# One of a step's three score maxima computed in two parts of 256 keys, one in either half of TensorE's array

## The chip, the cores and the metric

The kernel runs on one core of one Trainium2 chip. The metric is the device time of one execution in microseconds (us). Three runs of the kernel before the change took 1636.03, 1638.93 and 1639.0 us (median 1638.93). One further execution was profiled; every duration of an instruction below is from it.

Engines: TensorE (PE for its matmuls, PEld for its weight loads), VectorE (DVE), ScalarE (ACT), GpSimd (POOL), and SyncE (SP), which issues DMAs. Each takes its instructions in order from a queue of its own; across engines, semaphores order them. TensorE writes to PSUM, which has eight banks of 128 x 512 float32.

## The reference

Two attention layers over the same shapes, their outputs side by side. S = 2048 positions, D = 576, 32 heads of 18.

```python
def _B_ref(x, wqkv, wo):                      # full attention
    qkv = (x @ wqkv).reshape(B, S, 3, H, Dh).transpose(2, 0, 3, 1, 4)
    q, k, v = qkv[0], qkv[1], qkv[2]
    scores = einsum("bhqd,bhkd->bhqk", q, k) * Dh ** -0.5
    o = einsum("bhqk,bhkd->bhqd", softmax(scores), v)
    return o.transpose(0, 2, 1, 3).reshape(B, S, D) @ wo

def _A_ref(x, wqkv, wo):                      # each query sees 8 keys: itself, 2, 4, ... 14 back
    ...
    logits = where(mask, einsum("bhsd,bhswd->bhsw", q, kg) * Dh ** -0.5, -1e9)
    o = einsum("bhsw,bhswd->bhsd", softmax(logits), vg)
    return o.transpose(0, 2, 1, 3).reshape(B, S, D) @ wo

return concatenate([a, b], axis=-1)           # a = _A_ref, b = _B_ref
```

## The kernel before

**Attention B** takes nearly all of TensorE's time. The heads are worked in eight groups of four (`g`), the queries of a group in four blocks of 512 (`b`), the keys of a block in 16 tiles of 128 (`kt`). One (g, b, kt) is a *step*: 32 blocks x 16 = 512 steps. In a step `score` (L222) makes, for each of the four heads, the 128 x 512 scores of the key tile against the block's queries (a matmul, L229, over 56 rows) and lets ScalarE take their exponential out of PSUM into `e` (L235). One step later `weigh` (L697) multiplies the four `e` by the values (L700, eight passes in the trace) into `po`, one bank that gathers a block's 16 steps. Heads 0 and 2 have their queries and keys on partitions 0 to 63 (r = 0, the lower rows of TensorE's array), heads 1 and 3 on partitions 64 to 127 (r = 1, the upper rows). Matmuls in the two halves can run at the same time.

**The maxima.** The softmax subtracts each query's largest score. It comes in as two further rows of `qs`, hence 56 rows in L229, so a block's maxima must be known before its steps begin. They are made as a second product, over 54 rows with the queries as weights: `take` (L156) multiplies 128 queries by 512 keys into a bank (L159), `reduce` (L163) has VectorE reduce that bank to one column of `mx` (L166). A block needs 64 such pieces: 2 halves `r`, 2 heads `p` in each, 4 query tiles `t`, 4 key ranges `k`. When the last one is reduced, `least` (L170) reduces over `k` (L173), and `turn`, `halve` and `place` follow in later steps: a transposition on VectorE, a split on POOL (L104 and L105), DMAs into `qs`. The maxima of block n + 1 and later are made during the steps of block n: a block's maxima last about 21 steps. `maximum(r)` (L208) hands out the next piece of half `r`. Pieces of the first eight blocks are mostly made earlier, while the projections run (`stream`, L286).

**Order in a step.** `score` is called for h = 0, 1, 2, 3; with `also` true, a piece of the other half (1 - r) is issued behind the score's matmul and its reduction behind the exponential. `positions` picks the heads that get one: three as a rule, four where `behind()` finds the maxima late. With heads 0, 1 and 2 the queue of TensorE is: score r0, maximum r1, score r1, maximum r0, score r0, maximum r1, score r1, then the weighing. `inside` holds products of output projections (`sums_of_a`, `quarter`) that go in front of the third or fourth score; `beside` (L991), which makes them, also takes two pieces of maxima along while there are any.

**Banks.** Seven banks besides `po`: four in the ring "scores", three in the ring "else" (L80), from which the maxima take theirs in turn.

**Attention A** is made on POOL, between the steps, in eight chunks of 256 queries (`local`, L814). A dictionary `agenda` holds what is due at which step; chunk j's plan begins at step 10 + 54 j (L1086). Counted from there, the products `match` (L837, L841) are due at 5, 7, 10, 12, ... 25, the maximum over the window on VectorE (L855) at 31 to 33, `lower` (L861) at 33, the exponential on ScalarE (L864) at 35, sums and reciprocals on VectorE (L855, L871) at 36 to 39, `share` (L874) at 39, the weighted sums (L880 to L883) at 39, 41, 44, ... 59, then L887 at 60 and L892 at 61. Each `match` or weighted sum holds POOL for about 4.6 us. POOL also does the end of each of attention B's blocks (`finish`, L705: L736, L737, L738 at 18, 19 and 20 steps behind its end). What is due at the end of a step is put into the engines' queues there; each engine gets to it when it can.

Of the kernel before, what the change touches and what calls it, by code (L numbers as in the profile page):

```python
# [7 lines left out]
F32 = mybir.dt.float32  # L8
# [3 lines left out]
ALU = mybir.AluOpType  # L12
AX = mybir.AxisListType
# [9 lines left out]
NG = H // 4  # L23
NT = S // 128
NB = S // 512
SCALE = DH ** -0.5
MASKED = -1e9 / SCALE
LEAST = -3.0e38
AB = 256
NJ = S // AB  # L30
SUB = AB // 4
# [5 lines left out]
PIECES = 2 * 4 * NB  # L37
# [4 lines left out]
AHEAD = 7  # L42
# [9 lines left out]
def ap(t, *dims):  # L52

    return bass.AP(tensor=t.tensor, offset=t.offset, ap=[list(t.ap[0])] + [list(d) for d in dims])
# [8 lines left out]
def two_attentions(ctx: ExitStack, tc, xa, wa, woa, xb, wb, wob, out):  # L63
# [5 lines left out]
    nc = tc.nc  # L69
# [5 lines left out]
    maxes = ctx.enter_context(tc.tile_pool(name="maxes", bufs=1))  # L75
# [33 lines left out]
    step = 0  # L109

    def later(n, f):
        agenda[step + n].append(f)
# [5 lines left out]
    def due():  # L118
        for f in agenda.pop(step, []):
            f()  # L120
# [29 lines left out]
    def block(g, b):  # L150

        qs, ks = sets[g % 3]
        mx = maxes.tile([128, 2, 2, 4, NB], F32, name="mx", bufs=3)
        left = 2 * PIECES

        def take(r, t, k, p):  # L156
            ps = bank()
            at = slice(64 * r, 64 * r + 54)
            nc.tensor.matmul(ps, qs[at, b, p, 128 * t : 128 * t + 128],  # L159
                             ks[at, p, 512 * k : 512 * k + 512], start=True, stop=True)  # L160
            return ps

        def reduce(ps, r, t, k, p):  # L163
            nonlocal left
            left -= 1
            nc.vector.tensor_reduce(mx[:, r, p, t, k : k + 1], ps, axis=AX.X, op=ALU.max)  # L166
            if left == 0:
                least()

        def least():  # L170
            m = least_rooms[n_least[0] % 2]
            n_least[0] += 1
            nc.vector.tensor_reduce(m[:, :16], mx.rearrange("q r p t k -> q (r p t) k"), axis=AX.X, op=ALU.max,  # L173
                                    negate=True)
            later(1, lambda: turn(m))

        def turn(m):

            raw = maxes.tile([128, 32], F32, name="mt", bufs=2)
            nc.vector.transpose(raw, m)  # L180
            later(1, lambda: halve(raw))

        def halve(raw):
            mh = maxes.tile([128, 32], F32R, name="mh", bufs=2)
            split_on(nc.gpsimd, mh, raw.bitcast(F32R), raw)
            later(2 if g == NG - 1 else 5, lambda: place(mh, raw))

        def place(*parts):
            placed.add((g, b))
            for k, t in enumerate(parts):  # L190
                for j in range(4):
                    load(ap(qs.bitcast(F32)[54 + k : 128 : 64, b, 0, 32 * j :], (128, 8), (1, 32)),
                         t.bitcast(F32)[32 * j : 32 * j + 16])

        return take, reduce


# [6 lines left out]
    blocks = {}  # L204
    given = [0, 0]
    projecting = True

    def maximum(r):  # L208

        n, i = divmod(given[r], PIECES)  # L210
        given[r] += 1
        if n not in blocks:
            blocks[n] = block(*divmod(n, NB))
        take, reduce = blocks[n]
        piece = (r, i // 2 // NB, i // 2 % NB, i % 2)
        ps = take(*piece)
        return lambda: reduce(ps, *piece)

    e_room = None
    counted = [-1]  # L220

    def score(g, b, kt, h, also, kind="scores"):  # L222

        assert (g, b) in placed
        qs, ks = sets[g % 3]
        p, r = divmod(h, 2)
        ps = bank(kind)
        at = slice(64 * r, 64 * r + 56)
        nc.tensor.matmul(ps, ks[at, p, 128 * kt : 128 * kt + 128], qs[at, b, p], start=True, stop=True)  # L229
        reduce = maximum(1 - r) if also else None  # L230

        counted[0] += 1
        early = counted[0] % 8 < 6
        e = (e_room if early else work).tile([128, 512], F32, name="e", bufs=6 if early else 2)
        nc.scalar.activation(e, ps, AF.Exp, scale=SCALE)  # L235
        if reduce:
            reduce()
        return e

    vs = {}  # L240
# [45 lines left out]
    def stream(products, most, last):  # L286
# [9 lines left out]
        for j in range(len(products)):  # L296
# [42 lines left out]
    with (tc.tile_pool(name="x", bufs=1, side="right") as xp,  # L339
# [103 lines left out]
        if True:  # L443
# [34 lines left out]
            for c in range(5):  # L478
                one, other = (load, nc.scalar.dma_start) if c % 2 == 0 else (nc.scalar.dma_start, load)
# [11 lines left out]
            ahead = deque()  # L491
# [67 lines left out]
            for t in range(NT):  # L559
                ps = bank()  # L560
# [78 lines left out]
            for k in range(2, 14):  # L639
                n = 46 if k == 2 else 36 + 4 * k  # L640
# [14 lines left out]
            for t in order[:4]:  # L655
                ps = bank()
# [18 lines left out]
            for c, b in order:  # L675
                n = min(128, 3 * D - 128 * c)
                work_list.append(((b % 2, ws[c][0], xas[b][0], slice(0, n), every),
                                  lambda ps, n=n: ps[:n], lambda ps, c=c, b=b, n=n: leave_a(c, b, n, ps)))

            es = []  # L680
            few = 2 * (NT - 4)
            turns = len(work_list) - NT + 4
            stream(work_list, lambda j: 2 * (j + 1) if j < NT - 4 else
                   few + (EARLY_PAIRS - few) * (j - NT + 5) // turns,
                   [[lambda h=h: es.append(score(0, 0, 0, h, False, "else")) for h in (r, r + 2)] for r in range(2)])
        wa_room.close()

        over, agenda = agenda, defaultdict(list)
# [2 lines left out]
        step = 0  # L691
# [5 lines left out]
    def weigh(*steps):  # L697
        for g, b, kt, es in steps:
            for i in range(4):
                nc.tensor.matmul(po[32 * i : 32 * i + 19], vs[g][:, kt, 19 * i : 19 * i + 19], es[i],  # L700
                                 start=kt == 0, stop=kt == NT - 1)
        if kt == NT - 1:
            finish(g, b)
# [86 lines left out]
    producing = set()  # L790
# [196 lines left out]
    inside = []  # L987
# [115 lines left out]

    total = early + rest

    def behind():

        most = 0
        for n in range(sum(given) // (2 * PIECES), NG * NB):
            until = NT * n - AHEAD  # L1110
            more = 3 * (until - step) + 2 * sum(step <= p < until for p in producing)
            most = max(most, 2 * PIECES * (n + 1) - sum(given) - more)
        return most

    def positions(n):

        if n == 3:
            ahead = given[1] > given[0]
            return (0, 1, 3) if ahead else (0, 1, 2)
        if n == 1:  # L1120
            return (0,) if given[0] > given[1] else (1,)
        return range(4) if n > 3 else (0, 1) if n == 2 else ()

    paired = False
    due()
    step += 1
    while step < ALL:
        n, kt = divmod(step, NT)
        g, b = divmod(n, NB)
        places = positions(min(4 if behind() > 0 else 3, total - sum(given)))  # L1130
        es = []
        for h in range(4):

            if inside and h == (3 if 3 in places else 2):
                inside.pop(0)()
            es.append(score(g, b, kt, h, h in places))
        for fs in (behind_scores, outside):
            while fs:
                fs.pop(0)()

        paired = paired or kt % 2 == 0 and sum(given) == total
        for _ in range(1 if paired and step < ALL - 2 else len(waiting)):
            if waiting:
                waiting.pop(0)()
        if ready and (kt % 2 == 0 or not paired):
            weigh(ready.pop(0))
        ready.append((g, b, kt, es))
        if paired and kt % 2:
            weigh(*ready)
            ready.clear()  # L1150
        due()

        if len(waiting) > (0 if not paired else 2 if kt % 2 else len(waiting)):
            waiting.pop(0)()
        step += 1
# [24 lines left out]
```

## Time and profile before

| | us |
|---|---|
| median of three runs | 1638.93 |
| lowest, highest | 1636.03, 1639.0 |
| the profiled execution | 1637.69 |
| its span, first to last instruction | 1635.9 |

| engine | busy us | share of the span | instructions |
|---|---|---|---|
| TensorE, matmuls | 1627.4 | 99% | 12906 |
| TensorE, weight loads | 944.2 | 58% | 12906 |
| VectorE | 1393.1 | 85% | 2366 |
| ScalarE | 1223.1 | 75% | 2419 |
| POOL | 959.4 | 59% | 792 |

The costliest groups are the maxima's reductions (L166, 2048 of 684 ns), the exponentials (L235, 2048 of 608 ns), the maxima's matmuls (L159, 2048 of 422 ns), the scores' matmuls (L229, 2048 of 425 ns) and the weighing (L700, 4096 passes of 599 ns). A row of the timeline has the start in us from the span's start, the duration in us (from the first to the last of merged instructions), engine, line, operation, what is written and read by the program's names, the shapes and a count; in square brackets stands the idle time of the engine before it and what ended it. Matmuls overlap, so their durations do not add up; their starts are what to read. In a row of windows stand, for each engine, the busy time and number of instructions, then the granted TensorE clock (1.00 is full speed), and the share and rate of the DMA engines.

### The profile page before, as it was taken

How to read it: one execution, taken by the hardware profiler on the slowest of the kernel's cores; microseconds unless marked ns; L12 is line 12 of the kernel's file. 1: busy time of each engine (PE TensorE's matmuls, PEld its weight loads, DVE VectorE, ACT ScalarE, POOL GpSimd, SP SyncE). 2: the span in 40 equal slices, each digit the busy share in tenths (PEclk: the TensorE clock that was granted, in tenths of full speed). 3: DMA queues.
4: the chain of work that ended last, by engine and by line, in shares of the span. 5: the costliest groups of instructions: out<-in, count | busy, mean ns of one | idle time of the engine just before them, and what ended most of it. 6: DMA issues, size and time to landing. Idle time of an engine off the chain costs nothing.

```text
span 1635.9 us, 33786 instructions
## 1 busy us (share of the span) xinstructions
PE 1627.4 (99%) x12906; PEld 944.2 (58%) x12906; DVE 1393.1 (85%) x2366; ACT 1223.1 (75%) x2419; POOL 959.4 (59%) x792
## 2 busy tenths in 40 slices
PE   9999999999999999999999999999999999999998
PEld 7999888999433344444444444444444444444676
DVE  5199999999889899889889989899899899888533
ACT  6324432111899999999999999999999999998554
POOL 2306642210365996995994995995995997920000
PEclk9999999999999999999999999999999999999999
DMA  8937955522222253163135235332532151033201
GB/s 251 237 117 201 270 159 141 136 87 91 46 57 65 73 141 81 34 147 93 48 86 146 55 109 116 82 90 62 120 104 58 51 139 47 21 122 126 99 38 59
DMA packets 186050, 172.01 MB, mean 105 GB/s; under 512 B 119152, under 2 KB 132976, under 8 KB 184160
## 3 DMA queue, kind: packets, MB, share of 16 engines
q1 hardware_dynamic: 181024, 158.31, 34.9%
q0 software_dynamic: 4032, 10.63, 3.2%
q8 instruction: 101, 1.65, 0.5%
q10 hardware_dynamic: 832, 0.92, 0.2%
q14 instruction: 61, 0.50, 0.1%
HBM read 96.94 MB, written 71.90 MB: 103 GB/s over the span
## 4 chain that ended last, share of the span: by engine, by line
PE 96%; DMA 1%; POOL 1%; DVE 1%; issue 0%; ACT 0%; SPq 0%; POOLq 0%; ACTq 0%; DVEq 0%
PE po L700 31%; PE bank L229 25%; PE bank L322 14%; PE bank L159 14%; PE bank L1005 7%; PE bank L259 5%; DMA dqk<-olo 1%; POOL xlo L370 1%; PE bank L474 0%; DMA more<-xa 0%; DVE mx L166 0%; POOL olo L462 0%; DMA out<-y 0%; PE bank L980 0%; ACT vs L540 0%
## 5 line engine op out<-in xcount | busy, mean ns | idle before, releaser
L166 DVE TENSOR_REDUCE mx<-bank 128x1 f32<-128x512 f32 x2048 | 1288.1, 684 | 140.5 <-PE bank L159 113.3
L235 ACT ACTIVATE e<-bank 128x512 f32<-128x512 f32 x2048 | 1061.7, 608 | 87.1 <-PE bank L229 52.4
L159 PE MATMUL bank<-ks,qs 54*128 54x512 f32 x2048 | 750.5, 422 | 0.7 <-DVE mx L166 0.5
L229 PEld LDWEIGHTS bank<-qs,ks 56*128 56x128 f32 x2048 | 327.6, 185 | 446.5 <-ACT e L235 418.5
L229 PE MATMUL bank<-qs,ks 56*128 56x512 f32 x2048 | 571.3, 425 | 0.0
L700 PE MATMUL po<-e,v 128*19 128x512 f32 x4096 | 537.4, 599 | 0.0
L159 PEld LDWEIGHTS bank<-ks,qs 54*128 54x128 f32 x2048 | 340.1, 184 | 11.3 <-DVE mx L166 4.0
L700 PEld LDWEIGHTS po<-e,v 128*19 128x19 f32 x4096 | 70.6, 97 | 184.9 <-issue 182.1
L837 POOL TENSOR_TENSOR pr<-aq,akv 128x1024 f32<-128x1024 f32 x72 | 158.4, 2200 | 16.1 <-DMA akv<-da 13.5
L880 POOL TENSOR_TENSOR pr<-lg,akv 128x1024 f32<-128x1024 f32 x72 | 158.2, 2197 | 0.6
L841 POOL TENSOR_TENSOR pr<-pr 128x1024 f32<-128x1024 f32 x64 | 152.4, 2382 | 5.0
L650 ACT ACTIVATE ohi<-bank 128x512 f32<-128x512 f32 (+1 forms) x56 | 30.4, 595 | 151.0 <-issue 99.4
L322 PE MATMUL bank<-xhi,ahi 64*128 64x512 f32 (+1 forms) x448 | 114.6, 387 | 0.0
L322 PE MATMUL bank<-xhi,alo 64*128 64x512 f32 (+1 forms) x448 | 111.3, 387 | 0.0
L322 PE MATMUL bank<-xlo,ahi 64*128 64x512 f32 (+1 forms) x448 | 109.1, 388 | 0.1
L881 POOL TENSOR_TENSOR pr<-pr 128x512 f32<-128x512 f32 x72 | 92.3, 1283 | 5.6
L370 POOL TENSOR_TENSOR alo<-raw,ahi 128x512 fp32r<-128x512 f32 (+1 forms) x14 | 17.6, 1256 | 120.6 <-ACT ahi L369 93.7
L462 POOL TENSOR_TENSOR olo<-olo,ohi 128x512 fp32r<-128x512 f32 x36 | 46.1, 1294 | 66.3 <-ACT ohi L461 60.5
L736 POOL TENSOR_TENSOR o<-o,rec 128x512 f32<-128x512 f32 x29 | 37.4, 1289 | 59.7 <-ACT e L235 24.9
L322 PEld LDWEIGHTS bank<-xhi,ahi 64*128 64x128 f32 (+1 forms) x448 | 64.9, 181 | 3.0
L322 PEld LDWEIGHTS bank<-xhi,alo 64*128 64x128 f32 (+1 forms) x448 | 62.2, 182 | 2.9
L1005 PE MATMUL bank<-wohi,at 64*128 64x288 f32 x512 | 63.8, 295 | 0.0
(197 smaller groups left out, 1784.0 us busy)
## 6 DMA issues: line engine op xcount, KB each, us to landing
do<-n SPq DMA_DIRECT2D x28, 512.0 KB
da<-ohi SPq DMA_DIRECT2D x52, 256.0 KB
akv<-da SPq DMA_DIRECT2D x64, 175.5 KB
out<-y SPq DMA_DIRECT2D x32, 288.0 KB
qs<-dqk SPq DMA_DIRECT2D x30, 288.0 KB
ks<-dqk SPq DMA_DIRECT2D x30, 288.0 KB
at<-dao SPq DMA_DIRECT2D x64, 128.0 KB
rec<-drec SPq DMA_DIRECT2D x29, 256.0 KB
```

The source lines that it names most:

```text
L159: nc.tensor.matmul(ps, qs[at, b, p, 128 * t : 128 * t + 128], ks[at, p, 512 * k : 512 * k + 512], start=True, stop=True)
L166: nc.vector.tensor_reduce(mx[:, r, p, t, k : k + 1], ps, axis=AX.X, op=ALU.max)
L229: nc.tensor.matmul(ps, ks[at, p, 128 * kt : 128 * kt + 128], qs[at, b, p], start=True, stop=True)
L235: nc.scalar.activation(e, ps, AF.Exp, scale=SCALE)
L259: nc.tensor.matmul(ps, a, b, start=c == i == 0, stop=c == 4 and i == 1)
L322: nc.tensor.matmul(ps, a, b, start=start, stop=stop)
L700: nc.tensor.matmul(po[32 * i : 32 * i + 19], vs[g][:, kt, 19 * i : 19 * i + 19], es[i], start=kt == 0, stop=kt == NT - 1)
L837: nc.gpsimd.tensor_mul(pr, ap(st["q"][:, 2 * c], (SUB, 2), (0, W), (1, SUB)), window(st["k"], c))
L841: nc.gpsimd.tensor_add(st["pr"], st["pr"], pr)
L880: nc.gpsimd.tensor_mul(at, ap(st["lg"], (0, 2), (SUB, W), (1, SUB)), window(st["v"], c))
L881: nc.gpsimd.tensor_add(at[:, :, :4], at[:, :, :4], at[:, :, 4:])
L1005: nc.tensor.matmul(ps, a, b, start=start, stop=stop)
```

## The change

Each step now issues two whole pieces and one half of two others. `parts_of_maximum` takes one piece of either half of the array with the same `p`, `t`, `k`. In one step it multiplies the first 256 keys of both, in the next step the last 256. Both products of a step go into one bank, the piece of r = 0 into columns 0 to 255, that of r = 1 into 256 to 511, and one reduction of two rows of 256 reads them. The matmul of r = 1 is issued at the step's start. ScalarE gets a nop that waits for it, and the matmul of r = 0 waits for the nop.

The scores are issued in the order h = 0, 2, 1, 3. TensorE's queue in a step is: part r1, score r0, maximum r1, score r0, score r1, part r0, score r1, maximum r0, then the weighing. The two whole pieces are reduced right after the exponentials of h = 0 and h = 3, the parts after that of h = 1. `behind` and `positions` are gone; the total number of pieces is the same.

`mx` has a last dimension of 2 for the two parts. A whole piece writes only the first of the two, so `mx` is set to the least float32 on POOL when a block's first piece is handed out, and `LEAST` is changed for that. The reduction in `least` goes over eight values instead of four. In the built program the block's first reduction on VectorE waits for POOL's memset. `inside` now always goes in front of the fourth score.

```diff
-LEAST = -3.0e38
+LEAST = -3.4028234e38
...
-        mx = maxes.tile([128, 2, 2, 4, NB], F32, name="mx", bufs=3)
+        mx = maxes.tile([128, 2, 2, 4, NB, 2], F32, name="mx", bufs=3)
+        nc.gpsimd.memset(mx, LEAST)
...
-        def take(r, t, k, p):
-            ps = bank()
+        def take(ps, r, t, k, p, part=None):
             at = slice(64 * r, 64 * r + 54)
-            nc.tensor.matmul(ps, qs[at, b, p, 128 * t : 128 * t + 128],
-                             ks[at, p, 512 * k : 512 * k + 512], start=True, stop=True)
-            return ps
+            first, n = (0, 512) if part is None else (256 * part, 256)
+            return nc.tensor.matmul(ps if part is None else ps[:, 256 * r : 256 * r + 256],
+                                    qs[at, b, p, 128 * t : 128 * t + 128],
+                                    ks[at, p, 512 * k + first : 512 * k + first + n], start=True, stop=True)
...
+            if part is None:
+                ins = nc.vector.tensor_reduce(mx[:, r, p, t, k, :1], ps, axis=AX.X, op=ALU.max)
+            else:
+                ins = nc.vector.tensor_reduce(mx[:, :, p, t, k, part], ps.rearrange("q (r n) -> q r n", r=2),
+                                              axis=AX.X, op=ALU.max)
...
+    def next_piece(r):
         n, i = divmod(given[r], PIECES)
         given[r] += 1
         if n not in blocks:
             blocks[n] = block(*divmod(n, NB))
+        return blocks[n], (r, i // 2 // NB, i // 2 % NB, i % 2)
...
+    def parts_of_maximum():
+        if not begun:
+            both = [next_piece(r) for r in range(2)]
+            assert both[0][1][1:] == both[1][1][1:]
+            begun.extend((both, part) for part in range(2))
+        both, part = begun.popleft()
+        ps = bank()
+        one = both[1][0][0](ps, *both[1][1], part)
+        between = nc.scalar.nop()
+        sync(between, one)
+        def other():
+            (take, reduce), piece = both[0]
+            sync(take(ps, *piece, part), between)
+            reduce(ps, *piece, part)
+        return other
...
-        places = positions(min(4 if behind() > 0 else 3, total - sum(given)))
-        es = []
-        for h in range(4):
-            if inside and h == (3 if 3 in places else 2):
+        es = [None] * 4
+        whole = total - sum(given) > 1
+        parts = bool(begun) or total - sum(given) > 3
+        if parts:
+            part = parts_of_maximum()
+        for h in (0, 2, 1, 3):
+            if inside and h == 3:
                 inside.pop(0)()
-            es.append(score(g, b, kt, h, h in places))
+            es[h] = score(g, b, kt, h)
+            if h == 0 and whole:
+                maximum(1)()
+            if h == 1 and parts:
+                part()
+            if h == 3 and whole:
+                maximum(0)()
```

More of the change, by code (lines that the diff above doesn't have):

```diff
@@ L152, in block, with reduce @@
         qs, ks = sets[g % 3]
-        mx = maxes.tile([128, 2, 2, 4, NB], F32, name="mx", bufs=3)
+        mx = maxes.tile([128, 2, 2, 4, NB, 2], F32, name="mx", bufs=3)
+        nc.gpsimd.memset(mx, LEAST)
         left = 2 * PIECES
-        def take(r, t, k, p):
-            ps = bank()
+        def take(ps, r, t, k, p, part=None):
             at = slice(64 * r, 64 * r + 54)
-            nc.tensor.matmul(ps, qs[at, b, p, 128 * t : 128 * t + 128],
-                             ks[at, p, 512 * k : 512 * k + 512], start=True, stop=True)
-            return ps
-        def reduce(ps, r, t, k, p):
-            nonlocal left
+            first, n = (0, 512) if part is None else (256 * part, 256)
+            return nc.tensor.matmul(ps if part is None else ps[:, 256 * r : 256 * r + 256],
+                                    qs[at, b, p, 128 * t : 128 * t + 128],
+                                    ks[at, p, 512 * k + first : 512 * k + first + n], start=True, stop=True)
+        def reduce(ps, r, t, k, p, part=None):
+            nonlocal left
+            if part is None:
[3 more added lines that the diff above has]
+                                              axis=AX.X, op=ALU.max)
             left -= 1
-            nc.vector.tensor_reduce(mx[:, r, p, t, k : k + 1], ps, axis=AX.X, op=ALU.max)
             if left == 0:
                 least()
+            return ins
         def least():
@@ L172, in least @@
             n_least[0] += 1
-            nc.vector.tensor_reduce(m[:, :16], mx.rearrange("q r p t k -> q (r p t) k"), axis=AX.X, op=ALU.max,
+            nc.vector.tensor_reduce(m[:, :16], mx.rearrange("q r p t k s -> q (r p t) (k s)"), axis=AX.X, op=ALU.max,
                                     negate=True)
@@ L206, in two_attentions @@
     projecting = True
-    def maximum(r):
+    def next_piece(r):
         n, i = divmod(given[r], PIECES)
@@ L213, in maximum, with sync, score @@
             blocks[n] = block(*divmod(n, NB))
-        take, reduce = blocks[n]
-        piece = (r, i // 2 // NB, i // 2 % NB, i % 2)
-        ps = take(*piece)
-        return lambda: reduce(ps, *piece)
+        return blocks[n], (r, i // 2 // NB, i // 2 % NB, i % 2)
+    def maximum(r):
+        ps = bank()
+        (take, reduce), piece = next_piece(r)
+        take(ps, *piece)
+        return lambda: reduce(ps, *piece)
+    begun = deque()
+    def sync(ins, other):
+        tc.add_manual_dep(ins.ins, other.ins.name,
+                          mybir.DependencyInfo(mybir.DependencyClass.Sync, mybir.DependencyReason.DATA), reason="one bank")
+    def parts_of_maximum():
[4 more added lines that the diff above has]
+        both, part = begun.popleft()
+        ps = bank()
+        one = both[1][0][0](ps, *both[1][1], part)
[6 more added lines that the diff above has]
+        return other
     e_room = None
     counted = [-1]
-    def score(g, b, kt, h, also, kind="scores"):
+    def score(g, b, kt, h, kind="scores"):
         assert (g, b) in placed
@@ L229, in score @@
         nc.tensor.matmul(ps, ks[at, p, 128 * kt : 128 * kt + 128], qs[at, b, p], start=True, stop=True)
-        reduce = maximum(1 - r) if also else None
         counted[0] += 1
@@ L235, in score @@
         nc.scalar.activation(e, ps, AF.Exp, scale=SCALE)
-        if reduce:
-            reduce()
         return e
@@ L684, in two_attentions @@
                    few + (EARLY_PAIRS - few) * (j - NT + 5) // turns,
-                   [[lambda h=h: es.append(score(0, 0, 0, h, False, "else")) for h in (r, r + 2)] for r in range(2)])
+                   [[lambda h=h: es.append(score(0, 0, 0, h, "else")) for h in (r, r + 2)] for r in range(2)])
         wa_room.close()
@@ L1104, in two_attentions @@
     total = early + rest
[L1106 to L1122, printed above, removed]
     paired = False
@@ L1139, in two_attentions @@
                 fs.pop(0)()
-        paired = paired or kt % 2 == 0 and sum(given) == total
+        paired = paired or kt % 2 == 0 and sum(given) == total and not begun
         for _ in range(1 if paired and step < ALL - 2 else len(waiting)):
```

## The prediction

> **What bounds the kernel now.** I read the page first: busy shares, the slices, the chain that ended last.
>
> ```profile
> PE 1627.4 (99%) x12906; PEld 944.2 (58%) x12906; DVE 1393.1 (85%) x2366; ACT 1223.1 (75%) x2419; POOL 959.4 (59%) x792
> ...
> POOL 2306642210365996995994995995995997920000
> ...
> PE 96%; DMA 1%; POOL 1%; DVE 1%; issue 0%; ACT 0%; SPq 0%; POOLq 0%; ACTq 0%; DVEq 0%
> ```
>
> TensorE sets the end: busy in every slice, 96% of the chain. But POOL, 59% over the span, stands at 9 in two slices of three from the fourteenth on, so there it has hardly any room. A mean share hides that.
>
> Next, one step of the main loop in the timeline: TensorE, then ScalarE and VectorE (start, duration, both in us).
>
> ```profile
> 1002.23 0.50 PE L229 MATMUL bank<-qs,ks 56*128 56x512 f32 x1
> 1002.24 0.73 PE L159 MATMUL bank<-ks,qs 54*128 54x512 f32 x2
> 1002.58 0.63 PE L229 MATMUL bank<-qs,ks 56*128 56x512 f32 x2
> 1002.82 0.39 PE L159 MATMUL bank<-ks,qs 54*128 54x512 f32 x1
> 1003.05 0.39 PE L229 MATMUL bank<-qs,ks 56*128 56x512 f32 x1
> 1003.37 1.05 PE L700 MATMUL po<-e,v 128*19 128x512 f32 x8
> 1004.36 0.49 PE L229 MATMUL bank<-qs,ks 56*128 56x512 f32 x1
> ```
> ```profile
> 1002.77 1.09 ACT L235 ACTIVATE e<-bank 128x512 f32<-128x512 f32 x2
> ```
> ```profile
> 1003.26 1.08 ACT L235 ACTIVATE e<-bank 128x512 f32<-128x512 f32 x2
> ```
> ```profile
> 1003.74 1.10 ACT L235 ACTIVATE e<-bank 128x512 f32<-128x512 f32 x2
> ```
> ```profile
> 1002.80 0.69 DVE L166 TENSOR_REDUCE mx<-bank 128x1 f32<-128x512 f32 x1 [0.22 <-PE bank L159]
> ```
>
> A step lasts 1004.36 - 1002.23 = 2.13 us. Seven products over half of the array's rows start at 1002.23, 1002.58, 1002.82 (two each, one in either half) and 1003.05 (one alone), so a slot is 0.24 us and the fourth is half empty. The first slot, 0.35, holds 0.11 of loading weights. The weighing begins at 1003.37, 1.14 after the step's start and 0.32 after the lone product. Exponentials start 0.48 to 0.49 apart, so ScalarE could run a step in 4 x 0.48 = 1.92; three maxima cost VectorE 3 x 0.6 = 1.8. A step shorter than 1.92 is not to be had.
>
> **The change part by part.**
>
> *The empty half slot.* The new order is part one (upper rows, 256 keys), then seven whole or half products alternating between the halves: 3.5 slots in each. If all goes back to back, the last product starts at 0.11 + 2 x 0.24 + 0.12 = 0.71 and the weighing at 0.71 + 0.32 = 1.03: a gain of 0.11 a step. That is the upper bound of the gain.
>
> *The order by ScalarE.* Part two must wait for a nop in ScalarE's queue, and that nop for part one. A score needs 1002.77 - 1002.23 = 0.54 from its start to its exponential; part one streams half as long, so the nop can go at 0.54 - 0.12 = 0.42. The way from ScalarE back to TensorE is not seen alone. Its bounds are nothing and 0.19 (0.54 less 0.11 for weights and 0.24 for columns, the whole way in the other direction); I take half, 0.1, since no exponential is computed on it. Part two's weights then start at 0.52, its columns at 0.63 instead of 0.59, the last product at 0.63 + 0.12 = 0.75, the weighing at 1.07. The gain is 1.14 - 1.07 = 0.07 a step. Behind part two in TensorE's queue stand the fourth score, the last maximum and the weighing, so each late nop delays them all. Lower bound: the nop is served only when the fourth exponential of the step before is through. That one ends at 1003.74 + 1.10 = 1004.84, 0.48 into the next step, 0.55 with a step 0.07 shorter; with 0.1 back, 0.11 of weights and 0.12 + 0.32 behind it, the weighing starts at 1.20, a loss of 0.06. The nop itself lies in a pause: the next exponential cannot begin before 0.54.
>
> *VectorE.* Three reductions of 512 as before, one of them in two rows of 256: nothing. Part one's bank is read as second of three, at about 1.3 to 1.9 of the step, and is wanted first thing in the next step at 2.06, so some 0.15 us of slack is left. The wider final reduction (128 columns instead of 64) comes 32 times, once in a block, a few us at most on VectorE, which has 0.2 us idle a step: nothing.
>
> *The memset, on POOL.* Each of the 32 blocks now begins with a memset of `mx` in POOL's queue, and the block's first reduction waits for it. The cost itself is small; the nearest row is a memset of the same 128x128:
>
> ```profile
> L547 POOL MEMSET vs<- x4: 352/364/437, 51.5 to 79.6; 128x128 f32 x4
> ```
>
> What matters is what stands before it in POOL's queue: all that the steps before have handed POOL for attention A and for `finish`. Until now TensorE never had to wait for that work promptly. So I looked, for each block's start, at the last POOL operation handed over before it. A block ends on VectorE with L173 (0.2 us); its follower's first maximum comes right behind. Its long pauses are before L861 and L874, once in each of attention A's eight chunks (groups by form; the idle time before them is behind the bar):
>
> ```profile
> L861 POOL TENSOR_TENSOR lg<-lg,am 128x512 f32<-128x512 f32 x8 | 10.2, 1280 | 53.8 <-DVE am L855 53.8
> L874 POOL TENSOR_TENSOR lg<-lg,as 128x512 f32<-128x512 f32 x8 | 10.2, 1279 | 64.8 <-DVE as L871 52.7 <-ACT e L235 7.3 <-DMA aq<-da 4.6
> ```
>
> They part its work into eight stretches. Below is the block start in each where POOL lags most (blocks 12, 14, 17, 20, 22, 25, 28, 29), VectorE first, then POOL.
>
> ```profile
> 599.19 0.22 DVE L173 TENSOR_REDUCE m<-mx 128x16 f32<-128x64 f32 x1
> ...
> 692.87 0.22 DVE L173 TENSOR_REDUCE m<-mx 128x16 f32<-128x64 f32 x1
> ...
> 831.24 0.22 DVE L173 TENSOR_REDUCE m<-mx 128x16 f32<-128x64 f32 x1
> ...
> 970.29 0.22 DVE L173 TENSOR_REDUCE m<-mx 128x16 f32<-128x64 f32 x1
> ...
> 1063.59 0.22 DVE L173 TENSOR_REDUCE m<-mx 128x16 f32<-128x64 f32 x1
> ...
> 1201.43 0.22 DVE L173 TENSOR_REDUCE m<-mx 128x16 f32<-128x64 f32 x1
> ...
> 1341.29 0.22 DVE L173 TENSOR_REDUCE m<-mx 128x16 f32<-128x64 f32 x1
> ...
> 1388.64 0.22 DVE L173 TENSOR_REDUCE m<-mx 128x16 f32<-128x64 f32 x1
> ```
> ```profile
> 613.22 1.27 POOL L738 TENSOR_TENSOR n<-o,n 128x512 fp32r<-128x512 f32 x1
> ...
> 696.42 1.14 POOL L887 CAST aohi<-ao 128x1152 fp32r<-128x1152 f32 x1
> ...
> 835.43 2.39 POOL L841 TENSOR_TENSOR pr<-pr 128x1024 f32<-128x1024 f32 x1
> ...
> 976.52 2.39 POOL L841 TENSOR_TENSOR pr<-pr 128x1024 f32<-128x1024 f32 x1
> ...
> 1071.01 2.37 POOL L841 TENSOR_TENSOR pr<-pr 128x1024 f32<-128x1024 f32 x1
> ...
> 1205.07 2.38 POOL L841 TENSOR_TENSOR pr<-pr 128x1024 f32<-128x1024 f32 x1
> ...
> 1345.51 2.39 POOL L841 TENSOR_TENSOR pr<-pr 128x1024 f32<-128x1024 f32 x1
> ...
> 1394.05 0.46 POOL L883 TENSOR_TENSOR ao<-pr 128x128 f32<-128x128 f32 x1
> ```
>
> POOL's end less the next maximum (L173's start + 0.2): 15.1, 4.5, 6.4, 8.4, 9.6, 5.8, 6.4, 5.7; together 62. In a stretch POOL runs without a pause, so whatever TensorE waits at one block start is taken off the lag at the next; a stretch costs its largest lag, once. Each adds the memset's 0.36 and loses VectorE's slack of 0.15: 8 x 0.2 = 2, so 64. VectorE stands still through such a wait, all three maxima's banks are full after one more step, and the next step begins with part one, which needs one: TensorE stands, and ScalarE with it.
>
> From a stretch's L874 (step 49 + 54j) to its worst block (steps 85, 125, 187, 247, 288, 349, 410, 430) POOL sets the pace and a faster step wins nothing: 36 + 22 + 30 + 36 + 23 + 30 + 37 + 3 = 217 steps. Of 487 steps with parts 270 keep their gain: 270 x 0.07 = 19 us.
>
> *The early blocks.* While the projections run, blocks 1 and 2 start so:
>
> ```profile
> 125.14 0.22 DVE L173 TENSOR_REDUCE m<-mx 128x16 f32<-128x64 f32 x1
> ```
> ```profile
> 128.27 1.02 POOL L370 TENSOR_TENSOR wlo<-raw,whi 128x384 fp32r<-128x384 f32 x1
> ```
> ```profile
> 166.93 0.22 DVE L173 TENSOR_REDUCE m<-mx 128x16 f32<-128x64 f32 x1
> ```
> ```profile
> 173.32 0.60 POOL L143 DMA_DIRECT2D ks<-dqk  x1
> ```
>
> POOL is 129.29 - 125.3 = 4 and 173.92 - 167.1 = 6.8 late. Between nothing (TensorE has other products there) and both, 11; I take the larger alone, 7, as the first wait may count towards the second.
>
> *The clock.* After the last matmul the granted clock falls:
>
> ```profile
> 1625.00:1630.00 5.00, 4.60 (x33) 3.95 (x30) 4.32 (x12) 1.02 (x4) 1.83 (x4) 1.00 0.00 0
> 1630.00:1636.00 6.00, 1.16 (x9) 0.93 (x7) 1.32 (x4) 0.41 (x1) 0.00 (x0) 0.84 0.64 247
> ```
>
> TensorE ends 1.16 into the second window, and a mean of 0.84 over 6 us is full speed until 4.1 if the rest is at half: the clock falls 2.9 us after the work stops. How long it stays low with work back is not shown; bounds are nothing and, say, as long as it took to fall (an estimate), which loses 2.9 / 2 = 1.5 us. A stretch pays its lag in two or three pieces, not all over 2.9; with six long ones, 6 x 1.5 = 9 us. [...]
>
> *The sum*, on the profiled execution's own 1637.69 us (1.2 under the median): 1637.7 + 64 - 19 + 7 + 9 = **1699 us**, 3.7% slower. With the ideal gain of 0.11 it is 1688; with none, 1718.
>
> **The rivals.**
>
> 1. *POOL's wait is hidden*, and the change pays. It needs the memset to be done when the block starts. For it: at some starts POOL is ahead and idle, and POOL's spans are rough in a profile. Against: a queue runs in order, and in the quoted rows operations handed over earlier end 4 to 15 us after the block began. Then 487 x 0.07 = 34 us are won: 1604, or 1584 with the ideal gain. Chance 0.12, with 0.03 for a balance within what can be told apart, 0.2% or 3 us.
>
> 2. *The order by ScalarE is late as well* (the lower bound, 0.06 lost a step): every step longer, for one nop behind one exponential. For it: ScalarE is busy 9 tenths and more here. Against: exponentials start 0.48 apart and last 0.6, so its queue starts one before the other ends, and a nop should pass too. It decides as soon as the nop is served after 0.59 of the step. Outside the stretches 270 x 0.06 = 16 are lost instead of 19 won: 1734. Chance 0.10.
>
> 3. *The halves don't overlap* in TensorE (one bank, two row halves), so the half slot isn't saved: the 1718 of above. It stands within the forecast's case, 0.75 in all.
>
> **How the numbers follow.** Slower: 0.75 + 0.10 = 0.85; same 0.03; faster 0.12. The forecast's own range, from gain, clock and early bounds, is 1675 to 1725. Towards rival 2 and long clock losses I go to 1755; downwards to 1650, for stretches that POOL eats only half, leaving out rival 1.
>
> **What would show it.** Right: at block starts the first maximum waits 3 to 11 us for the memset, TensorE has pauses there (it has none now), POOL's L874 waits stay; between block starts a step takes 2.06. The clock dips behind the long pauses. Wrong: no idle of VectorE put down to the memset line; or a step over 2.13 between block starts with part two waiting for ScalarE; or pauses without a dip of the clock.

## The result and the profile after

The changed kernel takes 1735.22 us (median of four runs, 1733.23 to 1735.38) against 1638.97 us: 1.0587 times as long, 95% interval 1.0569 to 1.0606. The forecast was 1699 us, range 1650 to 1755. Sign and cause were right; the loss is 96 us and not 60.

The page of the changed kernel, engines and chain:

```profile
PE 1636.6 (94%) x13394; PEld 966.2 (56%) x13394; DVE 1394.6 (80%) x2366; ACT 1213.4 (70%) x2419; POOL 962.6 (56%) x824
...
PEclk9999999999999889999999899999999999899999
...
PE 54%; POOL 23%; DVE 6%; ACT 2%; DMA 2%; issue 2%; SPq 0%; POOLq 0%; DVEq 0%; ACTq 0%
```

POOL's busy time has not moved (962.6 us, it was 959.4), but 23% of the chain that ended last now runs through it; it was 1%. TensorE's clock, at 9 throughout before, shows slices at 8.

The waits of VectorE (in total, times, longest), and the start of block 22, for which the prediction worked out 9.6 us, in the timelines of TensorE, VectorE and POOL:

```profile
DVE mx L170 <- POOL mx L155: 80.4, 17, 7.6
```
```profile
1119.95 1.05 PE L737 MATMUL po<-e,v 128*19 128x512 f32 x8
1127.32 0.58 PE L162 MATMUL bank<-ks,qs 54*128 54x256 f32 x1 [6.32 <-DVE mx L172]
```
```profile
1118.71 0.68 DVE L170 TENSOR_REDUCE mx<-bank 128x1 f32<-128x512 f32 x1
1125.97 0.69 DVE L170 TENSOR_REDUCE mx<-bank 128x1 f32<-128x512 f32 x1 [6.58 <-POOL mx L155]
1126.58 0.68 DVE L172 TENSOR_REDUCE mx<-bank 128x2 f32<-128x512 f32 x1
```
```profile
1118.61 2.65 POOL L929 TENSOR_TENSOR ao<-ao,aohi 128x1152 fp32r<-128x1152 f32 x1
1121.22 2.16 POOL L874 TENSOR_TENSOR pr<-aq,akv 128x1024 f32<-128x1024 f32 x1
1123.46 2.34 POOL L878 TENSOR_TENSOR pr<-pr 128x1024 f32<-128x1024 f32 x1
1125.74 0.20 POOL L155 MEMSET mx<- 128x128 f32 x1
```

This is to be read from the bottom. POOL works through attention A's operations one behind the other and comes to the memset, of 0.2 us, at 1125.74. VectorE's reduction has waited 6.58 us for it. After it comes the parts' reduction (L172), and only that frees the bank which part one of the next step needs: TensorE stood for 6.32 us. The rest of the block's lag was paid in the block before, as the prediction said of a stretch (4.5 us there). Over the trace TensorE has 16 pauses of more than 1 us, 77 us in all (10 us of it in the two early blocks); before there was one, of 1.1 (a pause of 1.5 at the program's start, which every version has, is left out).

The granted clock around this pause (stretch and length, busy times of TensorE, its weight loads, VectorE, ScalarE and POOL, then the clock, DMA share and rate):

```profile
1121.00:1124.00 3.00, 0.00 (x1) 0.00 (x0) 0.00 (x0) 1.01 (x3) 2.92 (x3) 1.00 0.15 53
1124.00:1127.00 3.00, 0.00 (x0) 0.00 (x0) 1.02 (x2) 0.00 (x0) 3.00 (x3) 0.68 0.86 343
1127.00:1130.00 3.00, 2.68 (x20) 2.68 (x22) 2.44 (x5) 1.58 (x3) 2.92 (x2) 0.50 0.01 3
1130.00:1133.00 3.00, 3.00 (x29) 2.35 (x27) 1.80 (x3) 0.77 (x2) 1.77 (x2) 0.68 0.00 0
```

The clock is at half for 1.9 us of the second window, all of the third and 1.9 of the fourth: 6.8 us, most of it after the work is back.

Between the pauses a plain step (one without an output product) runs as forecast. TensorE's timeline:

```profile
1039.71 0.38 PE L162 MATMUL bank<-ks,qs 54*128 54x256 f32 x1
1039.71 0.49 PE L269 MATMUL bank<-qs,ks 56*128 56x512 f32 x1
1039.93 0.40 PE L162 MATMUL bank<-ks,qs 54*128 54x512 f32 x1
1040.05 0.51 PE L269 MATMUL bank<-qs,ks 56*128 56x512 f32 x2
1040.28 0.30 PE L162 MATMUL bank<-ks,qs 54*128 54x256 f32 x1
1040.40 0.44 PE L269 MATMUL bank<-qs,ks 56*128 56x512 f32 x1
1040.42 0.42 PE L162 MATMUL bank<-ks,qs 54*128 54x512 f32 x1
1040.77 1.05 PE L737 MATMUL po<-e,v 128*19 128x512 f32 x8
1041.76 0.38 PE L162 MATMUL bank<-ks,qs 54*128 54x256 f32 x1
```

A step is 1041.76 - 1039.71 = 2.05 us, the weighing starts 1.06 into it; it was 2.13 and 1.14 in the step shown of before. The halves do overlap: part two starts at 0.57, with the second score not yet through.

But other steps got longer, those with an output product by most. Matched one by one with the same steps of before (start of the first score to that of the next step's), steps with an output product of `beside` take 4.7 us and not 4.24. TensorE and VectorE in one of them:

```profile
1086.28 0.29 PE L162 MATMUL bank<-ks,qs 54*128 54x256 f32 x1
...
1087.08 0.30 PE L1042 MATMUL bank<-wolo,at 64*128 64x288 f32 x2
1087.70 0.50 PE L162 MATMUL bank<-ks,qs 54*128 54x512 f32 x1 [0.32 <-DVE mx L172]
```
```profile
1086.35 0.69 DVE L170 TENSOR_REDUCE mx<-bank 128x1 f32<-128x512 f32 x1 [0.15 <-PE bank L162]
1086.96 0.68 DVE L172 TENSOR_REDUCE mx<-bank 128x2 f32<-128x512 f32 x1
1088.23 1.99 DVE L170 TENSOR_REDUCE mx<-bank 128x1 f32<-128x512 f32 x3 [0.59 <-PE bank L162]
```

The first maximum inside the product takes the parts' bank. That is free only when L172 ends at 1087.64, so TensorE stops in the middle of the product, and VectorE then has nothing to do for 0.59 us.

### The profile page after: what moved, and what is told of

The parts are those of the page before. It is cut to its first block, busy times and chain, and to the rows that moved or that the text cites. A ratio compares the mean times of both kernels' runs of the same rounds, so it can differ in the third digit from the quotient of the medians.

```text
span 1733.3 us, 35285 instructions
## 1 busy us (share of the span) xinstructions
PE 1636.6 (94%) x13394; PEld 966.2 (56%) x13394; DVE 1394.6 (80%) x2366; ACT 1213.4 (70%) x2419; POOL 962.6 (56%) x824
## 4 chain that ended last, share of the span: by engine, by line
PE 54%; POOL 23%; DVE 6%; ACT 2%; DMA 2%; issue 2%; SPq 0%; POOLq 0%; DVEq 0%; ACTq 0%
PE po L737 17%; PE bank L359 12%; PE bank L162 11%; PE bank L269 10%; POOL pr L917 7%; PE bank L1042 5%; POOL pr L918 4%; DVE mx L170 3%; POOL pr L874 3%; POOL pr L919 2%; POOL pr L878 2%; DVE mx L172 2%; ACT e L274 2%; POOL ao L920 1%; POOL n L775 1%
## 5 line engine op out<-in xcount | busy, mean ns | idle before, releaser
L170 DVE TENSOR_REDUCE mx<-bank 128x1 f32<-128x512 f32 x1560 | 1033.2, 685 | 235.3 <-PE bank L162 128.9
L274 ACT ACTIVATE e<-bank 128x512 f32<-128x512 f32 x2048 | 1051.1, 608 | 174.6 <-PE bank L269 158.7
L162 PE MATMUL bank<-ks,qs 54*128 54x256 f32 (+1 forms) x2536 | 807.9, 385 | 89.1 <-DVE mx L172 77.3
L162 PEld LDWEIGHTS bank<-ks,qs 54*128 54x128 f32 x2536 | 421.4, 188 | 567.5 <-DVE mx L172 458.6
L269 PE MATMUL bank<-qs,ks 56*128 56x512 f32 x2048 | 580.0, 434 | 0.1
L737 PE MATMUL po<-e,v 128*19 128x512 f32 x4096 | 549.1, 611 | 0.0
L172 DVE TENSOR_REDUCE mx<-bank 128x2 f32<-128x512 f32 x488 | 332.9, 682 | 0.0
L269 PEld LDWEIGHTS bank<-qs,ks 56*128 56x128 f32 x2048 | 307.4, 189 | 14.4 <-issue 7.1
L104 POOL CAST mh<-mt 128x32 fp32r<-128x32 f32 x32 | 6.8, 212 | 134.2 <-DVE mt L189 134.2
L898 POOL TENSOR_TENSOR lg<-lg,am 128x512 f32<-128x512 f32 x8 | 10.2, 1280 | 103.8 <-DVE am L892 103.8
```

What stands on the lines that cost most here:

```text
L162: return nc.tensor.matmul(ps if part is None else ps[:, 256 * r : 256 * r + 256], qs[at, b, p, 128 * t : 128 * t + 128], ks[at, p, 512 * k ...
L170: ins = nc.vector.tensor_reduce(mx[:, r, p, t, k, :1], ps, axis=AX.X, op=ALU.max)
L172: ins = nc.vector.tensor_reduce(mx[:, :, p, t, k, part], ps.rearrange("q (r n) -> q r n", r=2), axis=AX.X, op=ALU.max)
```

## The experiments

**1. The memset on VectorE** (`vector_memset`).

```diff
-        nc.gpsimd.memset(mx, LEAST)
+        nc.vector.memset(mx, LEAST)
```

> The changed kernel with the memset of mx on VectorE, so that no reduction waits for POOL. Theory (the loss is POOL's queue in front of the memset, with the clock that falls in the pauses): the 16 long pauses of TensorE and the clock dips are gone, a plain step stays at 2.05 us instead of 2.12, a step with an output product stays at 4.7 instead of 4.24; 1639 - 453 x 0.07 + 34 x 0.47 + 32 short memsets of about 0.1 = 1626 us, 1615 to 1640. Rival (the order by ScalarE and the new order of products are the loss): it stays above 1700 us.

1637.45 us (12 runs, 1635.41 to 1639.45) against 1638.38: ratio 0.9995, 0.9987 to 1.0004. The theory on the pauses holds: one pause of more than 1 us is left (2.45), and 98 us of the changed kernel are gone. So all of the loss is the memset's wait for POOL with what follows from it. The pause that is left is a wait for POOL too, without the memset: VectorE comes to attention A's maximum over the window (L892), which needs POOL's L881; the parts' reduction stands behind it in the queue, and TensorE waits for that.

```profile
625.22 0.43 DVE L892 TENSOR_TENSOR am<-lg 128x256 f32<-128x256 f32 x1 [2.37 <-POOL lg L881]
```
```profile
626.90 0.38 PE L162 MATMUL bank<-ks,qs 54*128 54x256 f32 x1 [2.45 <-DVE mx L172]
```

The gain, though, was not the expected 12 us but nothing. Against before, the 380 steps without a product that came out under 2.1 us win 32.2 us, 35 product steps lose 17.8, the 73 others lose 13.8. (These "plain" steps are told from the others by how long they came out, not by a cause.) The last were not in the expectation. TensorE's waits name the bank again (total, times, longest):

```profile
PE bank L162 <- DVE mx L172: 16.6, 46, 2.5
```

But the bank is not all of it. Of the 13.8 us, 3.1 are the pause above with the dip of the clock behind it. Another 3.4 lie at the starts of 11 blocks: there the first score has four waits in TensorE's queue, 0.1 us each. Before, they were passed 1.5 us ahead, while the weighing ran; now they are passed only when part one runs, and the score starts up to 0.43 us behind part one instead of with it. The other 60 steps lose 7.4 us, 5.8 of it in 41 that hold an operation of VectorE besides the maxima.

**2. The memset alone, in the kernel before** (`old_with_memset`).

```diff
         mx = maxes.tile([128, 2, 2, 4, NB], F32, name="mx", bufs=3)
+        nc.gpsimd.memset(mx, LEAST)
```

> The kernel before with nothing but the memset of mx on POOL at each block's start. Theory (POOL's queue): pauses of 3 to 8 us at most block starts, some 65 us in the main loop and 10 in the projections, a dozen clock dips of 3 to 10 us that cost some 20: about 1730 us, 1705 to 1745. Rival (the memset alone is harmless, it is the new order that makes it late): under 1650 us.

1728.93 us (1726.77 to 1730.45), ratio 1.0552, 1.0537 to 1.0568. One line that sets 64 numbers in a partition costs 91 us without anything else of the change. VectorE's waits and one block start in it:

```profile
DVE mx L167 <- POOL mx L154: 66.3, 16, 7.7
```
```profile
1070.18 0.63 PE L230 MATMUL bank<-qs,ks 56*128 56x512 f32 x3
1073.66 0.79 PE L160 MATMUL bank<-ks,qs 54*128 54x512 f32 x1 [2.84 <-DVE mx L167]
1074.38 1.91 PE L701 MATMUL po<-e,v 128*19 128x512 f32 x8
```

TensorE's pauses over 1 us are 52 us in all, less than expected; why was not tested. Most of the other 39 us fits the clock: TensorE's is at half for 75 us, in 67 of which TensorE works, and half of 67, the most that this can cost, is 33. The last row shows it: the weighing takes 1.91 us instead of 1.05.

**3. The memset on POOL, one block ahead** (`memset_ahead`). `room_of_maxima` makes the tile and its memset as before.

```diff
-        mx = maxes.tile([128, 2, 2, 4, NB, 2], F32, name="mx", bufs=3)
-        nc.gpsimd.memset(mx, LEAST)
+        mx = rooms.pop((g, b), None) or room_of_maxima()
+        ahead = divmod(g * NB + b + 1, NB)
+        if ahead[0] < NG:
+            rooms[ahead] = room_of_maxima()
```

> The changed kernel with the memset left on POOL, but handed to it one block (some 16 steps, 33 us) before its block starts. Theory (it is the 4 to 15 us of work in front of it): the pauses are gone, as with VectorE, 1615 to 1640 us. Rival (a memset on POOL costs wherever it stands, by its semaphore or by contention for memory): it stays above 1700 us.

1634.77 us (10 runs, 1633.02 to 1636.1), ratio 0.9976, 0.9967 to 0.9985. The same memsets on the same engine now cost nothing that can be seen; it was the work in front of them. One pause is left here too, of 3.1 us, at the same place as in experiment 1.

**4. The maxima later in the product** (`later_pairs`, on top of experiment 1).

```diff
-                turns[r].insert(6 + 4 * r, None)
+                turns[r].insert(11 + r, None)
```

> As vector_memset, and in a step with an output product the two pieces of maxima come behind 11 and 12 of its matmuls instead of 6 and 10. Theory (the first of them waits 0.6 us for the parts' bank, whose reduction is second in VectorE's queue): such a step takes 4.2 instead of 4.7 us, 34 x 0.5 = 17 us less than vector_memset, about 1609. Rival (VectorE has too much to do in such a step, so the pause only moves to the next bank): within 4 us of vector_memset.

1639.75 us, ratio 1.0009, 1.0001 to 1.0018, 2 us from experiment 1: the rival's outcome. Product steps take 4.75 to 4.8 us. TensorE and VectorE in one:

```profile
955.51 0.50 PE L162 MATMUL bank<-ks,qs 54*128 54x512 f32 x1 [0.26 <-DVE mx L170]
955.94 1.05 PE L737 MATMUL po<-e,v 128*19 128x512 f32 x8
```
```profile
953.42 0.68 DVE L172 TENSOR_REDUCE mx<-bank 128x2 f32<-128x512 f32 x1
954.77 1.97 DVE L170 TENSOR_REDUCE mx<-bank 128x1 f32<-128x512 f32 x3 [0.67 <-PE bank L162]
```

TensorE no longer stops for the parts' bank inside the product. But the two maxima now come later, VectorE idles 0.67 us for them, and the step's last maximum waits 0.26 us for the next bank instead. The hole has only moved.

**5. The nop behind the first exponential** (`later_nop`, on top of experiment 1). `order` issues the nop that waits for part one.

```diff
-        between = nc.scalar.nop()
-        sync(between, one)
...
             es[h] = score(g, b, kt, h)
+            if h == 0 and parts:
+                order()
```

> As vector_memset, but the nop stands behind the step's first exponential in ScalarE's queue instead of in front of it. Theory (part two is just in time: the nop runs at 0.42 of the step, its columns start at 0.57 when the score before it ends; any delay of the nop delays the last maximum and the weighing): the nop runs at 0.54 or later, a plain step takes 2.13 to 2.16 instead of 2.05 us, 453 x 0.1 = 45 us less some 10 that VectorE's lateness no longer costs, about 1672, 1660 to 1695. Rival (there is slack behind the nop, the step's end is set by something else): within 4 us of vector_memset.

1669.89 us, ratio 1.0187, 1.0168 to 1.0207, 2 us from the number expected. The nop runs at 0.42 of a step in the changed kernel and at 0.54 here (its sequencer event: 1040.13 in the step from 1039.71; 1032.77 in the step from 1032.22). A plain step takes 2.14 us. So part two had no slack: the 0.12 us by which the nop is later come out at the step's end as 0.1.

**6. The parts later in the step** (`part_last`, on top of experiment 3). These lines take the place of the loop over h; `score` calls `behind` right after its matmul, where part one and the nop are issued, and `made.pop()()` issues part two and the reduction.

```diff
+        made, part = [], parts and pieces_of_parts()
+        es[0] = score(g, b, kt, 0)
+        if whole:
+            maximum(1)()
+        es[2] = score(g, b, kt, 2, behind=parts and (lambda: made.append(parts_of_maximum(*part))))
+        es[1] = score(g, b, kt, 1)
+        last = maximum(0) if whole else None
+        es[3] = score(g, b, kt, 3)
+        if made:
+            made.pop()()
+        if last:
+            last()
+        if inside:
+            inside.pop(0)()
```

> As memset_ahead, with the parts moved within the step: part one third in the upper half's turn (score, maximum, score, part one, score, maximum, score, part two, weighing), reduced before the last maximum; an output product stands at the step's end instead of in front of the fourth score. Theory (the parts' bank, wanted first thing in a step and freed only just before, is what costs 0.5 us in product steps and 0.2 in those where VectorE has other work; and part two need not wait): plain steps 2.00 to 2.02 us instead of 2.05, the bank has 0.4 us to spare, product steps under 4.6; about 1605 us, 1595 to 1622. Rival (ScalarE's or VectorE's rate per step holds it, 1.9 and 1.8 us and what comes on top): no better than 1628 us.

1675.12 us, ratio 1.0219, 1.0202 to 1.0237: a miss. The rival's number holds, but not its reason, as experiment 7 shows. The half about the bank came true (a step with other work on VectorE is no longer slower than its neighbours: 426 of the 488 steps lie between 2.12 and 2.18 us), but the half about part two did not:

```profile
1082.69 0.50 PE L281 MATMUL bank<-qs,ks 56*128 56x512 f32 x1
...
1083.02 0.39 PE L281 MATMUL bank<-qs,ks 56*128 56x512 f32 x1
1083.03 0.28 PE L171 MATMUL bank<-ks,qs 54*128 54x256 f32 x1
...
1083.56 0.38 PE L171 MATMUL bank<-ks,qs 54*128 54x256 f32 x1
1083.86 1.06 PE L751 MATMUL po<-e,v 128*19 128x512 f32 x8
```

Part one (1083.03) is 0.12 us long in columns, but its nop ran at 1083.49, 0.46 after its start (its sequencer event, from the view by line):

```profile
L261 ACTq EVENT_SEMAPHORE  x1: 17/17/17, 1083.5 to 1083.5; - x1
```

A whole product in its place would need about that: the 0.31 us that part one takes in experiment 7, and 0.12 more for its other 256 columns.

**7. Part one in front of the second score** (`part_third`).

```diff
         if whole:
             maximum(1)()
-        es[2] = score(g, b, kt, 2, behind=parts and (lambda: made.append(parts_of_maximum(*part))))
+        if parts:
+            part = parts_of_maximum(*part)
+        es[2] = score(g, b, kt, 2)
...
+        if inside:
+            if parts:
+                part()
+            inside.pop(0)()
+            es[3] = score(g, b, kt, 3)
+            if whole:
+                maximum(0)()
```

> As part_last, but part one stands in front of the second score in TensorE's queue instead of behind it; product steps have part two in front of the product and the last maximum behind the fourth score again. Theory (in part_last the nop ran at 0.80 of the step, not 0.66, because TensorE reports a matmul's end no earlier than the ends of those queued ahead of it, and the second score ended 0.12 behind part one): the nop runs at 0.65, part two's columns start at 0.83, a plain step takes 2.00 to 2.04 us; about 1605 us, 1590 to 1622. Rival (the nop waited for its turn behind the exponential in ScalarE's queue): it still runs at 0.8, plain steps 2.13 to 2.17, 1650 to 1680 us.

1621.17 us (1619.08 to 1622.66) against 1637.93: ratio 0.9901, 0.9884 to 0.9917. The nop runs at 0.65 of a step (1042.45 in the step from 1041.80), as the theory had it:

```profile
1041.80 0.49 PE L281 MATMUL bank<-qs,ks 56*128 56x512 f32 x1
...
1042.14 0.28 PE L171 MATMUL bank<-ks,qs 54*128 54x256 f32 x1
...
1042.64 0.28 PE L171 MATMUL bank<-ks,qs 54*128 54x256 f32 x1
1042.86 1.05 PE L748 MATMUL po<-e,v 128*19 128x512 f32 x8
```
```profile
L261 ACTq EVENT_SEMAPHORE  x1: 17/17/17, 1042.5 to 1042.5; - x1
```

Part one starts at the same 0.34 of the step as in experiment 6; only its place in the queue against the second score differs, and the nop comes 0.15 earlier. That holds over all 488 steps: the nop runs 0.31 us behind part one's start here (median; nine in ten under 0.32), 0.46 there. Plain steps take 2.04 us, product steps 4.33. Against before, 402 plain steps win 33.4 us, product steps lose 10.2 and the others 5.3, where experiment 1 lost 17.8 and 13.8. The four waits at block starts are passed ahead again, as a score now stands first in the step. Of the 10.2 us, 4.8 fall in one step, in which TensorE pauses for 3.3 us at the place known from experiment 1; a usual product step is 0.1 us longer than before. This version is faster than both kernels, by 1% than the one before. It came out at the slow end of the expected range, 16 us above its middle figure: the product steps stayed above 4.24 us, and the pause with its dip remains.

## Why the prediction was right, and where its sizes were off

**POOL's queue.** Right in mechanism and size: 64 + 7 us of pauses were predicted, 77 were seen. Experiments 1 to 3 leave no other cause: without POOL in front, or with the memset early enough, the pauses are gone but for one of another origin, and the memset alone makes them in the old kernel. Rival 1, the hidden wait, is out. That a stretch pays its lag once is borne out in the eight stretches: their pauses sum to 14.0, 5.6, 5.3, 9.0, 10.9, 5.1, 9.8 and 7.4 us, where 15.1, 4.5, 6.4, 8.4, 9.6, 5.8, 6.4 and 5.7 were predicted. That the sums agree so well is in part luck: a dip of the clock inside a stretch gives POOL time too, and the prediction kept the two apart.

**The order by ScalarE.** Right: nop at 0.42, weighing at 1.06 (1.07 predicted), 0.07 us a step. That the total fits so well is partly luck: part two's columns start at 0.57 and not at 0.63, but the last product follows 0.14 behind them and not 0.12, and the weighing 0.35 behind that and not 0.32. Rival 2 is out for the change as it stands, but experiment 5 shows that its price was real and its margin nothing. The 0.59 of a step from which the prediction lets rival 2 decide does not follow from its own sum, which breaks even with the nop at 0.49 (1.14 less 0.1, 0.11, 0.12 and 0.32); in experiment 5 a nop at 0.54 makes a step of 2.14, about what it was before.

**The overlap of the halves.** Rival 3 is out: the half slot is saved.

**VectorE and the parts' bank: the step that failed.** The prediction put this at nothing, with "some 0.15 us of slack". The slack is right for a plain step (L172 ends 0.1 us before part one wants the bank), but where the product takes the same bank it is overrun, and often also where VectorE has one operation more. In experiment 1 the product steps lose 17.8 us and the others 13.8, together as much as all plain steps win; the rows show the bank for the product steps, while of the 13.8 some 6 us go with VectorE's further operations, and the rest has the causes named there. That part one in first place delays a block's first score was not in the prediction either. In the changed kernel itself the 453 steps of the main loop without a pause or a dip win 10 us in all: 31 in 372 plain ones, less 16 in product steps and 6 in the others. The term of -19 us should have been -10.

**The clock.** Right in mechanism, mis-sized: 9 us for six long pauses. There are 14 dips in the changed kernel. Its difference to experiment 1 is 1735.2 - 1637.5 = 97.8 us; 77 less the one pause that experiment 1 has too are 74.5, so some 23 us are left for the dips. That is a little low, as experiment 1 has a dip of its own. Against before, the 35 steps of the main loop that hold a pause or a dip are 92 us longer, 67 of it pauses: 25 us for 12 dips. The part ahead of the main loop, with the other two, is 14 us longer, 9 of it pauses. So the dips cost some 30 us, 2 a dip. What one costs was not far off (1.5); how many pauses are long enough was.

Together: 5 us more of pauses (77 less the one of 1.1 that was there before, against 71), 21 of clock and 9 of gain that was not there make 35, against the 36 by which the forecast was short.

## What to carry to other kernels

An instruction that costs 0.2 us costs what stands in front of it in its engine's queue when something urgent waits for it. Before giving a small task to an engine with a long backlog, compare the end of what was handed over earlier with the time at which the result is wanted; then hand it over earlier (one block ahead sufficed here) or to the engine that waits for it. And when a result is put together from two products in one bank, count the bank as taken from the first product to the end of its reduction: the place in the step where it is wanted next decided more here than the matmul time saved: moving part one, with the memset ahead in both, took the ratio from 0.9976 to 0.9901.

## What the runs showed of the hardware

How soon part one's nop ran depended on what stood in front of part one in TensorE's queue, though that ran in the other half of the array: right behind a score twice as long, part one's nop ran 0.46 us after its start (experiment 6), and 0.31 us when it stood ahead of that score (experiment 7). The 0.15 us between them is near the 0.12 by which the score's columns end later, as the theory of experiment 7 has it; these two runs are all that shows it.

The clock fell here when the work was already back. TensorE at the end of a pause in the changed kernel, and the windows around it:

```profile
1021.35 0.38 PE L162 MATMUL bank<-ks,qs 54*128 54x256 f32 x1 [3.08 <-DVE mx L172]
...
1022.38 1.68 PE L737 MATMUL po<-e,v 128*19 128x512 f32 x8
```
```profile
1018.30:1021.30 3.00, 0.00 (x0) 0.00 (x0) 1.30 (x3) 0.38 (x1) 3.00 (x3) 1.00 0.00 0
1021.40:1022.60 1.20, 1.20 (x12) 0.79 (x16) 1.09 (x2) 0.72 (x2) 1.12 (x2) 1.00 0.00 0
1022.80:1026.00 3.20, 3.20 (x20) 1.51 (x16) 2.50 (x6) 2.33 (x6) 1.74 (x1) 0.50 0.11 35
```

It stands at full speed through the pause of 3.08 us and for 1.2 us of work behind it; then it is at half, and the weighing that runs across the fall takes 1.68 us instead of 1.05.

Whether a pause cost clock depended on when it fell. All falls and returns of the clock within the span of this trace stand whole multiples of 3.41 us apart, and the 14 dips last 3.4, 6.8 or 10.2 us. Cut along these points (and leaving out the first 3.4 us), the trace shows, at full clock, a fall behind each stretch of 3.41 us in which TensorE was busy for 1.61 us or less, and none behind one with 1.78 or more. A pause of 1.78 us in it, ended at 1272.55, is divided 1.08 to 0.70 between two stretches, with 2.33 and 2.71 us of work, and none follows:

```profile
1268.44:1271.85 3.41, 2.33 (x20) 0.88 (x16) 1.37 (x4) 2.82 (x6) 3.33 (x4) 1.00 0.44 60
1271.85:1275.26 3.41, 2.71 (x23) 1.47 (x23) 3.27 (x7) 2.17 (x5) 3.33 (x2) 1.00 0.00 0
```

Of the pause of 2.45 us in experiment 1, 1.7 lie in one stretch, with 1.67 us of work, and a dip follows (the granted clock of the whole execution is 0.997 there):

```profile
625.21:628.62 3.41, 1.67 (x18) 1.36 (x18) 3.40 (x7) 1.42 (x4) 0.00 (x0) 1.00 0.40 116
```

So the 2.9 us that the prediction read from the program's end are no fixed delay: in the changed kernel the 14 falls come 1.8 to 5.1 us after the start of their pause.
